# The second input load moved from SyncE's DMA queue to ScalarE's at the start of a depthwise-separable convolution kernel

## The chip, the cores and the metric

The kernel runs on one core of a Trainium2 chip. The metric is the device time of one execution in microseconds (us); lower is better. TensorE does the matmuls, VectorE and ScalarE move and convert data, GpSimd does a few small copies, and SyncE issues most of the DMAs. DMAs of SyncE and of ScalarE stand in two queues of their own, q1 and q10 in the profile.

## The reference

The inputs are x (1, 384, 384, 384) in bf16, a depthwise filter dw (1, 1, 384) and a pointwise matrix pw (384, 384). With a filter of one tap the padding is zero, and what is computed is a scaling of each channel and a matrix product:

```python
out = x * dw[0, 0][None, None, None, :]
return jnp.einsum('bhwc,cd->bhwd', out, pw)
```

So the kernel multiplies 147,456 rows of 384 channels by one 384 x 384 matrix whose rows have been scaled by dw. It reads and writes about 113 MB each.

## The kernel before, in words

**Tiling.** The rows are cut into 288 *supertiles* of 512 rows. Supertiles are loaded in *chunks*: the first five chunks hold 1, 1, 2, 2 and 4 supertiles, then 26 chunks hold 10 each, and the last ones get small again. A chunk t is loaded by one DMA, `load_x(t)` (line 134), and x0, x1, x2 in the text are the chunks 0, 1, 2. The loads of a chunk of one supertile have 384 KB. Chunks belong to groups (the first five are group 0), and each group uses one of three input buffers `Xs` in turn. Each of the first five chunks has a place of its own in the first buffer, and a semaphore of its own (`s_x[0][0]` to `s_x[0][4]`), so the first five loads wait for nothing.

**What is done to a supertile.** VectorE transposes it in two halves into a buffer T (line 365): for each half it does one 32 x 32 block transpose of pairs of bf16. TensorE then does 48 matmuls of 32 rows by 384 columns (line 226, in four row groups at the same time) into four PSUM banks `PS[s]`, and ScalarE copies the four banks to an output buffer O (line 425). SyncE stores the outputs (line 174). There are two T buffers and two sets of PSUM banks, used in turn.

**Weights, at the start.** `pw` is loaded by SyncE in two DMAs (lines 181 and 182: rows 0 to 127, then rows 128 to 383). ScalarE's queue loads `dw_row` (line 179) and, in `touched` (line 180), four bytes of every fourth row of x0. TensorE turns dw into a column and multiplies pw by selection matrices that hold it (line 276, k = 0, 1, 2, two results r each, the two of k = 2 with some matmuls repeated). The six results are converted to `w_r` by casts (line 381): the second by VectorE, the five others by ScalarE. TensorE runs some matmuls on constants before and between (line 243). The matmuls of line 226 begin when three of ScalarE's casts and VectorE's one are done, and the first half of x0 is transposed:

```python
w_first = {(0, 0): [(0, 1), (1, 3)], (4, 0): [(1, 4)], (4, 1): [(1, 5)]}
```

ScalarE's own order at the start is: issue `dw_row`, issue `touched`, load its activation table and write two small `warm` copies (line 342, they also release the two PSUM sets for the first time), then the casts, then the output copies.

**Order of the DMAs on SyncE.** It is written out by a sorted list `todo`, in which each entry has the supertile after which it is due; loads of the first three groups have -1 and come at once, in the order of the chunks. Before chunk 5 (the first one of 10 supertiles) SyncE waits until x1 has landed, and before the first store it has 28 waits that are long fulfilled. The semaphore `s_x` of a chunk is raised by its DMA whatever queue issued it, and VectorE waits for it before the first transpose of the chunk.

Of the kernel before, what the change touches and what calls it, by code (L numbers as in the profile page):

```python
# [26 lines left out]
def kernel(  # L27
# [12 lines left out]
    nc = tc.nc  # L40
# [19 lines left out]
    NT = len(chunks)  # L60
# [53 lines left out]
    with tc.tile_critical(sync_engine=mybir.EngineType.Pool, no_gpsimd_drain=True):  # L114
        def x_of(t):
            g, i, off, first, L = chunks[t]
            if first + 2 == NS:
                return Xl[:], s_xl, 32
            n = sum(len(ls) > i for ls in groups[g % NR : g + 1 : NR])
            return Xs[g % NR][:, 4 * off : 4 * (off + L), :], s_x[g % NR][i], 16 * n  # L120

        def load_x(t, eng=nc.sync):
            g, i, off, first, L = chunks[t]
            dst, sem, _ = x_of(t)
            rows = xf[512 * first : 512 * (first + L), :]
            if first + 3 < NS:
                src = rows.rearrange("(p s) c -> p (s c)", p=P)
                dst = dst.rearrange("p s c -> p (s c)")
                if i == 0 and g >= NR:
                    je = g_end[g - NR]  # L130
                    eng.wait_ge(s_t[je % 2][1], je // 2 + 1)
            else:
                src = rows.rearrange("(a k q) c -> q a k c", k=4, q=4)
            eng.dma_start(dst, src).then_inc(sem, 16)
# [46 lines left out]
        nc.sync.dma_start(pw_n[:, 0], pw[0:P, :]).then_inc(s_pw, 16)  # L181
        nc.sync.dma_start(pw_n[:, 1:3], pw[P:C, :].rearrange("(k p) d -> p k d", p=P)).then_inc(s_pw2, 16)
        load_x(0)

        todo = []
        for t, (g, i, off, first, L) in enumerate(chunks):
            if 0 < t < NT - 2:
                todo.append((g_end[g - NR] if g >= NR else -1, load_x, (t,)))
            for k in range(n_parts[t] - (first + 1 == NS)):
                todo.append((first + L * (k + 1) // n_parts[t] + 1, store, (t, k)))  # L190
# [275 lines left out]
```

## Time and profile before

| | |
|---|---|
| median of 4 runs | 573.96 us (573.54 to 574.03) |
| the profiled execution, its own time | 575.26 us |
| span of the profiled execution, first to last instruction | 573.2 us |
| mean granted TensorE clock | 0.999 |
| TensorE busy | 568.0 us (99%) |
| VectorE busy, ScalarE busy | 507.4 us (89%), 418.8 us (73%) |
| DMA queue of SyncE (q1) | 25796 packets, 225.91 MB, 97.5% of 16 engines' span |
| DMA queue of ScalarE (q10) | 1078 packets, 0.89 MB, 0.5% |

The span runs from the first to the last instruction of the profiled execution. Rows of the profile give a line of the kernel, an engine, an operation, its output and input, and a count; then the busy time, the mean duration of one in ns, and the idle time of the engine just before it with what ended that idle time. In the timeline each row begins with its start and its duration in us. An engine with "q" behind its name (SPq, ACTq) is the queue in which it issues DMAs; such a row is the issue, not the transfer. The time of a transfer is given as "us to landing", from the start of its issue.

### The profile page before, as it was taken

Reading aid. Unit: us, or ns where it says so; the run is one execution under the profiler, and the core shown is the slowest. Engines: PE = TensorE matmul, PEld = TensorE weight load, DVE = VectorE, ACT = ScalarE, POOL = GpSimd, SP = SyncE. Lnnn points to the kernel's source line nnn. Section 1 sums busy time; section 2 is a strip of 40 time slices with the busy share of each in tenths; the row PEclk is TensorE's granted clock in tenths of the full one; section 3 lists DMA queues with packets and bytes.
Section 4 is the critical chain, followed back from the end, with each engine's and each line's share of the span. In section 5 each row is a group of like instructions: output and inputs, shape, how many; then the busy total and the mean of one; then the engine's idle time right before and its main releaser. Section 6 shows DMA issues by size and latency. Waiting matters only on the chain.

```text
span 573.2 us, 29707 instructions
## 1 busy us (share of the span) xinstructions
PE 568.0 (99%) x13843; PEld 383.5 (67%) x13843; DVE 507.4 (89%) x586; ACT 418.8 (73%) x298; POOL 13.9 (2%) x41
## 2 busy tenths in 40 slices
PE   8999999999999999999999999999999999999997
PEld 4666666666666666666666666666666666666664
DVE  6898889889889889988988988988898898898885
ACT  6777777777777777777777777777777777777775
POOL 2042000000000000000000000000000000000000
PEclk9999999999999999999999999999999999999999
DMA  8999999999999999999999999999999999997877
GB/s 325 440 391 425 420 417 426 441 415 414 420 416 397 388 398 426 402 389 401 426 400 383 416 415 406 390 420 412 393 399 426 398 386 404 420 396 303 338 288 262
DMA packets 26884, 226.88 MB, mean 396 GB/s; under 512 B 1529, under 2 KB 7418, under 8 KB 23034
## 3 DMA queue, kind: packets, MB, share of 16 engines
q1 hardware_dynamic: 25796, 225.91, 97.5%
q10 hardware_dynamic: 1078, 0.89, 0.5%
q14 instruction: 9, 0.07, 0.0%
q8 instruction: 1, 0.02, 0.0%
HBM read 113.54 MB, written 113.25 MB: 396 GB/s over the span
## 4 chain that ended last, share of the span: by engine, by line
PE 99%; DMA 1%; ACT 0%; issue 0%; SPq 0%; POOLq 0%
PE ps L226 98%; DMA raw<-in_pw_dram 1%; PE ps L276 0%; PE ps L311 0%; PE ps L299 0%; ACT O L420 0%; SPq L181 0%; SPq L461 0%; POOLq L114 0%; POOLq L450 0%
## 5 line engine op out<-in xcount | busy, mean ns | idle before, releaser
L226 PE MATMUL ps<-w_r,T 32*128 32x384 bf16 x13776 | 560.8, 322 | 0.1
L365 DVE STREAM_TRANSPOSE T<-X 128x384 uint32<-128x384 uint32 x572 | 500.1, 875 | 57.4 <-DMA X<-in_x_dram 2.0
L425 ACT CAST O<-ps 128x1536 bf16<-128x1536 f32 x286 | 411.7, 1440 | 147.4 <-PE ps L226 147.4
L226 PEld LDWEIGHTS ps<-w_r,T 32*128 32x128 bf16 x13776 | 380.6, 93 | 180.6 <-issue 0.7
L340 POOL COPY Xk<-Xl 32x256 bf16<-32x256 bf16 x16 | 6.3, 394 | 0.0
L339 POOL COPY Xk<-Xl 32x128 bf16<-32x128 bf16 x16 | 4.6, 287 | 24.4 <-DMA Xl<-in_x_dram 23.5
L381 ACT CAST w_r<-ps 128x768 bf16<-128x768 f32 x5 | 3.7, 810 | 0.9 <-PE ps L276 0.9
L334 POOL COPY raw<-w_r 32x768 bf16<-32x768 bf16 x4 | 3.3, 819 | 6.9 <-ACT w_r L381 6.8
L276 PE MATMUL ps<-raw 64*128 64x384 bf16 x16 | 2.9, 516 | 0.5 <-DMA raw<-in_pw_dram 0.4
L243 PE MATMUL ps<-const-bfloat16-1.0 32*128 32x384 bf16 x24 | 2.2, 515 | 1.1 <-PEq L450 1.1
L342 ACT ACT_TABLE_LOAD x1 | 1.3, 1283 | 1.9 <-issue 1.9
L276 PEld LDWEIGHTS ps<-raw 64*128 64x128 bf16 x16 | 0.9, 126 | 2.5 <-DMA raw<-in_pw_dram 1.9
L416 DVE CAST O<-ps 128x384 bf16<-128x384 f32 x2 | 1.0, 552 | 1.4 <-PE ps L226 1.4
L365 DVE STREAM_TRANSPOSE T<-Xl 128x384 uint32<-128x384 uint32 x2 | 1.7, 872 | 0.2
L243 PEld LDWEIGHTS ps<-const-bfloat16-1.0 32*128 32x128 bf16 x24 | 0.7, 117 | 1.4 <-issue 1.4
L353 DVE STREAM_TRANSPOSE T<-Xk 128x384 uint32<-128x384 uint32 x2 | 1.2, 578 | 0.5 <-PE ps L226 0.4
L386 DVE TENSOR_REDUCE sel<-eye 128x64 f32<-128x128 bf16 x1 | 0.3, 289 | 1.5 <-POOL eye L321 1.5
L311 PE MATMUL ps<-raw,T 128*128 128x384 bf16 x8 | 1.5, 328 | 0.0
L420 ACT CAST O<-ps 128x384 bf16<-128x384 f32 x2 | 1.0, 478 | 0.7 <-PE ps L311 0.7
L381 DVE CAST w_r<-ps 128x768 bf16<-128x768 f32 x1 | 1.0, 958 | 0.5 <-PE ps L276 0.5
L420 DVE CAST O<-ps 128x384 bf16<-128x384 f32 x2 | 1.1, 558 | 0.1
L415 ACT CAST O<-ps 128x384 bf16<-128x384 f32 x2 | 0.9, 482 | 0.5 <-PE ps L226 0.5
(13 smaller groups left out, 4.5 us busy)
## 6 DMA issues: line engine op xcount, KB each, us to landing
X<-in_x_dram SPq DMA_DIRECT2D x26, 3840.0 KB, 21.3
out_dram<-O SPq DMA_DIRECT2D x26, 3840.0 KB, 27.3
X<-in_x_dram SPq DMA_DIRECT2D x3, 1536.0 KB, 18.0
out_dram<-O SPq DMA_DIRECT2D x4, 768.0 KB, 7.5
out_dram<-O SPq DMA_DIRECT2D x2, 1536.0 KB, 13.0
X<-in_x_dram SPq DMA_DIRECT2D x1, 2304.0 KB, 19.6
out_dram<-O SPq DMA_DIRECT2D x1, 2304.0 KB, 10.6
X<-in_x_dram SPq DMA_DIRECT2D x4, 384.0 KB, 4.7
```

What stands on the lines that cost most here:

```text
L226: mm = nc.tensor.matmul(PS[s][:, q, :D], lhsT=Ts[s][32 * q : 32 * q + 32, b, par::2], rhs=w_r[32 * q : 32 * q + 32, b, par, :], start=(b, ...
L243: nc.tensor.matmul(PS[0][:, 2 * (i % 2) + i // 2, :D], lhsT=ones[32 * i : 32 * i + 32, 0:P], rhs=ones[32 * i : 32 * i + 32, :], start=True ...
L276: mm = nc.tensor.matmul(PS[(k + 1) % 2][:, 2 * r + v, :D], lhsT=sel_w[64 * v : 64 * v + 64, k, r, :, :].rearrange("p q w -> p (q w)"), rhs ...
L311: mm = nc.tensor.matmul(PS[1][:, m, :D], lhsT=Tk[:, P * (m + 2) : P * (m + 3), par], rhs=w_k[:, par, :], start=False, stop=par == 1,)
L334: nc.gpsimd.tensor_copy(w_k[quads[n]], w_r[quads[n], n]).then_inc(s_wk)
L339: nc.gpsimd.tensor_copy(Xk[quads[n], g:8:4, :], x_b).then_inc(s_xk)
L340: nc.gpsimd.tensor_copy(Xk[quads[n], 8 + g : 24 : 4, :], Xl[quads[g], :, 64 * n : 64 * n + 64]).then_inc(s_xk)
L342: nc.scalar.copy(warm[:, s : s + 1], nc.const_aps.tensor(0.0, [P, 1], F32)).then_inc(s_a[s])
L365: ins = nc.vector.transpose(out=Tw[:, 3 * h : 3 * h + 3], in_=Xw[:, :, j, 96 * h : 96 * h + 96].rearrange("p k (b w) -> p b k w", w=32),)
L381: o = nc.vector.tensor_copy(out, in_) if e == 0 else nc.scalar.copy(out, in_)
L420: o = (nc.scalar.copy if n % 2 else nc.vector.tensor_copy)(Ov[:, n, j, :], PS[s][:, n, :D])
L425: a = nc.scalar.copy(Ov[:, :, j, :], PS[s][:, :, :D])
```

## The change

The load of chunk 1 is taken out of the sorted list on SyncE and issued on ScalarE, as its third instruction of the kernel, behind `dw_row` and `touched` and ahead of the table load. `load_x` already has the engine as an argument. The destination, the source and the semaphore are the same.

```diff
         load_x(0)
+        load_x(1, nc.scalar)
 
         todo = []
         for t, (g, i, off, first, L) in enumerate(chunks):
-            if 0 < t < NT - 2:
+            if 1 < t < NT - 2:
                 todo.append((g_end[g - NR] if g >= NR else -1, load_x, (t,)))
```

## The prediction

> **What bounds the kernel now.** I read the page's engine and chain parts first, then the chain in order of time, because its start shows what the change can touch. From the page:
>
> ```profile
> span 573.2 us, 29707 instructions
> ...
> PE 568.0 (99%) x13843; PEld 383.5 (67%) x13843; DVE 507.4 (89%) x586; ACT 418.8 (73%) x298; POOL 13.9 (2%) x41
> ...
> PE 99%; DMA 1%; ACT 0%; issue 0%; SPq 0%; POOLq 0%
> ...
> L226 PE MATMUL ps<-w_r,T 32*128 32x384 bf16 x13776 | 560.8, 322 | 0.1
> L365 DVE STREAM_TRANSPOSE T<-X 128x384 uint32<-128x384 uint32 x572 | 500.1, 875 | 57.4 <-DMA X<-in_x_dram 2.0
> ```
>
> TensorE is the bound. Its main line, L226, runs 560.8 us and stood idle 0.1 us in all. VectorE waited for x in 2.0 us only, three times (the waits table), all in the first 10 us. So x is never late for TensorE, and the change can act only on when the L226 run starts, on how fast its first microseconds go, and on the tail. Next, the chain in order of time:
>
> ```profile
> 1.41 3.16 DMA raw<-in_pw_dram
> 4.58 0.05 issue
> 4.62 2.10 PE ps L276 x12
> 6.72 0.08 issue
> 6.81 560.81 PE ps L226 x13189
> ```
>
> The start at 6.81 hangs on the second weight load (pw rows 128 to 383), not on x. Then the timeline of the first 8 us (start, duration):
>
> ```profile
> 0.96 0.54 ACTq L179 DMA_DIRECT2D dw_row<-in_dw_dram  x1
> 1.53 0.37 ACTq L180 DMA_DIRECT2D touched<-in_x_dram  x1
> 1.88 1.41 SPq L134 DMA_DIRECT2D X<-in_x_dram  x3
> 1.93 1.28 ACT L342 ACT_TABLE_LOAD   x1 [1.93 <-issue]
> 3.23 0.28 ACT L342 COPY warm<-const-float32-0.0 128x1 f32<-128x1 f32 x2
> 3.91 0.80 ACT L381 CAST w_r<-ps 128x768 bf16<-128x768 f32 x1 [0.39 <-PE ps L276]
> 5.16 1.50 ACT L381 CAST w_r<-ps 128x768 bf16<-128x768 f32 x2 [0.46 <-PE ps L276]
> 5.53 1.04 DVE L365 STREAM_TRANSPOSE T<-X 128x384 uint32<-128x384 uint32 x2 [0.34 <-DMA X<-in_x_dram]
> 7.06 1.04 DVE L365 STREAM_TRANSPOSE T<-X 128x384 uint32<-128x384 uint32 x2 [0.50 <-DMA X<-in_x_dram]
> ```
>
> L226 needs three ScalarE casts of weights; the third ends at 5.16 + 1.50 = 6.66, and TensorE starts 0.15 later. It also needs the first transposed half of x0: x0 lands about 5.5, half of 1.04 later it is 6.05. So x0 has about 0.6 us of slack. x1 is transposed from 7.06, its first half ready at 7.6. TensorE needs it after the first supertile, near 9.9 (ScalarE's first output cast starts at 9.97). So x1 has 2.3 us to spare: getting it earlier buys nothing by itself.
>
> **What the Trainium skill says.** "DMA: Bandwidth & Descriptors", section "Issuing engines are not separate DMA queues": transfers issued by different engines run on the same 16 DMA engines and interleave; only issue time is saved. Section "Queues, rings and completion order" of the same page: each engine goes round robin between its queues. The trace agrees as far as it shows. In the window 3.41 to 3.70 us, while both queues had work:
>
> ```profile
> q1 hardware_dynamic: 63, 0.08, 107.3%
> q10 hardware_dynamic: 62, 0.00, 12.0%
> ```
>
> 63 packets of SyncE's queue and 62 of ScalarE's (the tiny "touched" reads) went in the same 0.29 us. ScalarE's queue did not wait for SyncE's. "TensorE: Matmul & The Clock Gate", Part 1: matmuls run at half clock until a busy window of about 3.4 us has passed. The trace agrees: L226 matmuls take 516 ns on average in the window 6.8 to 8.1 and 321 ns in 9.3 to 11.0, with the first short ones near 8.8.
>
> **The change, part by part.**
>
> *SyncE.* One issue goes: three issues took 1.41, so 0.47 each, and x2, x3 and x4 are issued 0.47 sooner. They remain behind x0 in SyncE's queue, and the total bytes ahead of x2's end are the same, so x2 lands where it did (transposed from 9.24, needed near 9.9 + 1.95 = 11.9). x5 still waits on SyncE for x1, 2.7 us in the trace. It can move by about 0.5 either way, hidden by x4 ahead of it, 1536 KB issued near 1.88 + 4 × 0.47 = 3.8 and landing 11.5 later. Stores come after 11.4. Cost 0.
>
> *ScalarE.* One issue is added between "touched" and the table load. No row shows this issue on ScalarE early; its neighbours are 0.37 to 0.54, and the late ScalarE load of the same 384 KB takes 0.65. I take 0.4. Then the table load starts at 2.3, the warm copies end at 3.9, and the first weight cast starts at about 3.95 for 3.91. That cast ends at 4.75; the next one waits for TensorE until 5.16. The slack is 0.39 before the first cast plus 5.16 − 4.71 = 0.45 after it: 0.84 in all. At 0.4 the cost is 0; at 0.65 still 0. Queued behind the issue are the table load, the two copies that release PSUM, and the casts; no new semaphore wait is added.
>
> *DMA, the second weight load.* It lands at 4.57. x1 would be issued at 1.93, and x0, issued at 1.88, moves its first packets at about 3.4 (of the 125 packets in the window above, 109 are under 2 KB, so 16 are x0's). In 3.88 to 4.22 the trace has 15 packets under 2 KB, 6 of them under 512 B: 9 weight packets still to go. A 3 KB packet of x1 takes 3072 B at 396/16 = 24.8 GB/s, 0.124 us. If each of the nine were held up by one, the delay is 1.1; if x1 arrives after them, 0. "touched" takes the first five turns, so I take 0.3.
>
> *DMA, x0.* Alone in the queue it lands at 1.88 + 3.6 = 5.5; x1 follows at about 7.05, so a load of this size takes 1.0 (at 396 GB/s) to 1.5. Interleaved from the start, x0 ends nearly where the pair ends: later by 0 (x1 arrives late) to 1.5 (x1 wholly ahead). I take 1.0. Its first half is then transposed at 7.05, TensorE starts at about 7.2, and x0 has become the last wait. x1 lands near 6.8 or before and is queued on VectorE behind x0's transposes, ready near 8.1: in time.
>
> *Sum.* Start = the later of weights (6.81 + 0.3) and x0 (6.66 + 0.4 + 0.15): 0.4 later. While TensorE is at half clock until about 8.8 whatever it does, a late start of 0.4 loses work worth only 0.2; if the clock's rise moves along, 0.4. I take **0.3**. The profiled execution's span is 573.2 (its own time 575.26, 1.3 above the median), so the span after would be about 573.5; the median 573.96 becomes **574.3**. The end is not touched: the last stores follow the last matmuls.
>
> **Rivals.**
>
> *No change (573.9 to 574.1).* The change need not make the loads run side by side: x1's packets are behind "touched", and if descriptors for the two queues are made one after the other, x0 is nearly through first. For it: x0's slack of 0.6 and the weights' earlier issue. Against it: the equal packet counts above.
>
> *Clock not raised (slower, 576.0).* In the stretch from 2.0 to 5.4 TensorE waited 0.43 for the second weights and stayed at half clock; in 5.4 to 8.8 it waited 0.09 before L226 and the clock rose. If x0 becomes late by more than its slack, that gap grows to about 0.4, as long as the one that went with a cold clock. If the rise then fails, another window of 3.4 us runs at half rate (rows every 0.32 for 0.16), and costs half of it: 1.7, plus 0.3. It decides from the point where x0 lands later than about 6.2. Against it: if the weights are late by as much, the gap falls before the matmuls of L276 and not behind them.
>
> *ScalarE becomes the bound (slower, 574.8 to 575.1).* An issue of x on SyncE took up to 1.97 (the maximum of line 134; its median is 0.35). Such an issue on ScalarE, 1.1 past the slack of 0.84, shifts every weight cast by 1.1: 0.6 to 1.1. Against it: the first issues of x in this trace are short.
>
> *Faster (573.0).* Only 293 GB/s flowed in 3.4 to 5.5. If two queues fill this better, or if the clock rises earlier by a shift of its window, the gain is at most the half-clock part of L226: 6.81 to 8.8, half of 2.0, 1.0. Nothing in the change brings the weights sooner.
>
> **How the numbers follow.** 0.2% is 1.15 us, about what a measurement of this kernel can tell from no change. Likeliest case 0.53 (574.0 to 574.9), no change 0.20, clock 0.14, ScalarE 0.07, faster 0.06. Slower by over 0.2% is all of the clock case, half of ScalarE's and a tail of the likeliest, 0.20; faster by over 0.2%, 0.04, since its ceiling is 1.0; the rest, 0.76, is the same. The range 573.2 to 576.0 leaves out the larger half of the clock case and the faster case, some 0.13, and the bounds of x0 (to 1.5) and weights (to 1.1) fit in it.
>
> **What would show it.** ScalarE's queue has a third early issue of about 0.4 and the table load starts near 2.3; SyncE's L134 run has one issue fewer. x0's transposes start near 6.5 for 5.53 and x1's directly behind. The second weights' matmuls start 4.6 to 4.9, L226 near 7.1 to 7.2. The third cast still ends by 7.0. The first short L226 matmul is near 8.8; near 12 it is the clock case. I am wrong if L226 starts at 6.8 or before, if it has idle time past its start, or if the median moves by over 1.15 with the start where I put it.

## The result and the profile after

The change made the kernel slower by about 0.1%: the median went from 574.09 us (63 runs) to 574.63 (42 runs), and the ratio of the times is 1.0013 with a 95% interval of 1.0007 to 1.0018, so 0.4 to 1.0 us. That is below the 0.2% at which the prediction drew its line, and beyond what noise explains. The profiled execution took 574.53, with a span of 572.4.

The single times say more than the median. Of the 63 runs of before, 11 lie over 575.0; of the 42 after, 17 do. Below 575.0 the medians are 574.06 and 574.49, so 0.43 apart; of the 17 upper times of after, 13 lie between 575.9 and 577.3, some 1.7 above the lower ones. The means, which count the upper times in full, are 574.36 and 575.09, so 0.73 apart. So two things changed: all executions became a little later, and a second cluster of times became more frequent. The experiments look for a cause of each.

The page after, engines and the costliest group:

```profile
span 572.4 us, 29707 instructions
...
PE 566.2 (99%) x13843; PEld 417.1 (73%) x13843; DVE 507.4 (89%) x586; ACT 418.3 (73%) x298; POOL 13.9 (2%) x41
...
L227 PE MATMUL ps<-w_r,T 32*128 32x384 bf16 x13776 | 559.8, 321 | 1.2 <-DVE T L366 1.2
```

All lines below the added one are one higher now: L226 has become L227. Its idle time went from 0.1 to 1.2 us, and what ended it is VectorE's transpose. All of that wait lies ahead of its first matmul. The chain in order of time says the same:

```profile
1.88 4.39 DMA X<-in_x_dram
6.27 0.02 issue
6.29 0.59 DVE T L366
6.88 0.09 issue
6.97 559.83 PE ps L227 x13776
```

In place of the weight load, the load of x0 now heads the chain. The timeline of the same execution:

```profile
1.93 0.44 ACTq L134 DMA_DIRECT2D X<-in_x_dram  x1
2.41 1.28 ACT L343 ACT_TABLE_LOAD   x1 [2.41 <-issue]
...
3.91 0.80 ACT L382 CAST w_r<-ps 128x768 bf16<-128x768 f32 x1
...
4.42 1.32 PE L277 MATMUL ps<-raw 64*128 64x384 bf16 x12 [0.23 <-DMA raw<-in_pw_dram]
6.29 1.96 DVE L366 STREAM_TRANSPOSE T<-X 128x384 uint32<-128x384 uint32 x4 [1.10 <-DMA X<-in_x_dram]
```

ScalarE's table load is 0.48 later and its first cast still at 3.91, as forecast. x0's transposes start at 6.29, and x1's follow with no wait between. In the window 3.9 to 5.5 us the two queues share the DMA engines about evenly (packets, MB, share of the 16 engines' time):

```profile
q10 hardware_dynamic: 100, 0.31, 56.1%
q1 hardware_dynamic: 103, 0.28, 44.6%
```

One trap: the span fell from 573.2 to 572.4, while the kernel became slower. The profiled execution of before (575.26) was one of its upper times, the one after was a lower one. Two single profiles can't be subtracted as they stand, and the experiments therefore begin with what a usual execution of before looks like.

### The profile page after: what moved, and what is told of

Read it like the earlier page. It is cut to its first block, busy times and chain, and to the rows that moved or that the text cites. A ratio compares the mean times of both kernels' runs of the same rounds, so it can differ in the third digit from the quotient of the medians.

```text
span 572.4 us, 29707 instructions
## 1 busy us (share of the span) xinstructions
PE 566.2 (99%) x13843; PEld 417.1 (73%) x13843; DVE 507.4 (89%) x586; ACT 418.3 (73%) x298; POOL 13.9 (2%) x41
## 4 chain that ended last, share of the span: by engine, by line
PE 98%; DMA 1%; SPq 0%; DVE 0%; issue 0%; ACT 0%; POOLq 0%
PE ps L227 98%; DMA X<-in_x_dram 1%; PE ps L312 0%; PE ps L300 0%; DVE T L366 0%; ACT O L421 0%; SPq L182 0%; SPq L181 0%; SPq L462 0%; POOLq L114 0%; POOLq L451 0%
## 5 line engine op out<-in xcount | busy, mean ns | idle before, releaser
L227 PE MATMUL ps<-w_r,T 32*128 32x384 bf16 x13776 | 559.8, 321 | 1.2 <-DVE T L366 1.2
L227 PEld LDWEIGHTS ps<-w_r,T 32*128 32x128 bf16 x13776 | 414.6, 93 | 146.5 <-issue 1.6
```

The costliest lines, as they stand in the source:

```text
L227: mm = nc.tensor.matmul(PS[s][:, q, :D], lhsT=Ts[s][32 * q : 32 * q + 32, b, par::2], rhs=w_r[32 * q : 32 * q + 32, b, par, :], start=(b, ...
```

## The experiments

Theories. **Sharing**: x0 lands late because x1's packets take turns with its own, and TensorE waits for x0. Rivals: **issue**, that the added DMA issue ahead of ScalarE's table load costs; **queue**, that a load on ScalarE's queue costs by being there. For the upper times: **clock**, that TensorE's half clock goes on for another window when it idles too long ahead of its main matmuls, against **late transfer**, that in these executions some load comes later still.

| kernel | x0's transposes start | main matmuls start | full clock from | its own time | median us (runs) | over 575.0 |
|---|---|---|---|---|---|---|
| before, first profile | 5.53 | 6.81 | 8.86 | 575.26 | 574.09 (63) | 11 |
| before, second profile (e5_before) | 5.72 | 6.40 | 7.20 | 574.25 | 574.07 (13) | 2 |
| the change | 6.29 | 6.97 | 4.78 | 574.53 | 574.63 (42) | 17 |
| the change, e9_look1 | 6.28 | 6.96 | 10.91 | 576.40 | | |
| the change, e9_look2 | 6.20 | 6.88 | 5.79 | 574.55 | | |
| e2_issue | 5.36 | 6.38 | 4.82 | 573.86 | 573.83 (21) | 1 |
| e3_x1_first | 7.40 | 8.08 | 6.01 | 575.55 | 576.33 (11) | 9 |
| e1_apart | 6.25 | 6.93 | 6.14 | 575.34 | 575.84 (7) | 7 |
| e4_apart2 | 5.37 | 6.29 | 6.86 | 573.73 | 574.30 (14) | 2 |
| e6_fill | 6.37 | 7.05 | 5.08 | 574.38 | 574.75 (22) | 10 |
| e8_fill128 | 6.64 | 7.32 | 6.46 | 574.88 | 574.44 (13) | 3 |
| e7_nofill | 5.59 | 6.27 | 9.33 | 575.15 | 574.47 (14) | 5 |
| e10_before_fill | 5.44 | 6.68 | 6.60 | 574.54 | 574.19 (13) | 0 |

Columns two to five are of one profiled execution, which can be a slow or a quick one of its kernel; the last two are of all its runs. "Full clock from" is where the one long full-speed stretch begins in the trace's record of the granted clock. The record has no entry ahead of that stretch, so the page's PEclk doesn't show the half clock at the start. Each group of runs had runs of the kernel before beside it, and the ratios are against these. Over 575.0 were 11 of 63, 5 of 34, 3 of 51, 0 of 17 and 1 of 17 of them, so shares of different groups have to be compared with care.

**What a span is made of.** Take from a span the start of the main matmuls and half of the time from there to full clock. In eleven of the thirteen profiles 565.4 to 565.6 us are left: 572.42 − 6.97 in the change, 572.27 − 6.40 − 0.40 in the second profile of before, 574.33 − 6.96 − 1.98 in e9_look1. The other two (e1_apart, e10_before_fill) have a gap later in the main matmuls, of 0.42 at 11.0 and of 0.46 at 26.4. So in the profiles of the change the start and the clock are the whole loss, and a rival has to act through one of them.

**A usual execution of before.** The kernel is unchanged.

> The kernel before, unchanged, for a second profile. Clock theory: the first profile of it (its own time 575.26) had a late second weight load and a late rise of the clock, and is one of the few upper times. A usual execution (574.0) has its second weights by 4.4, x0's transposes directly behind VectorE's cast near 5.3, L226 starting at 6.4 to 6.6 and no long L226 matmul. Rival: it looks as the first profile does, start at 6.8 and long matmuls until 8.8.

The timeline of TensorE and of VectorE in this second profile (574.25 us, span 572.3):

```profile
3.37 2.94 PE L276 MATMUL ps<-raw 64*128 64x384 bf16 x16
...
6.40 5.92 PE L226 MATMUL ps<-w_r,T 32*128 32x384 bf16 x132
...
5.72 1.04 DVE L365 STREAM_TRANSPOSE T<-X 128x384 uint32<-128x384 uint32 x2 [0.53 <-DMA X<-in_x_dram]
```

The second weights came in time: the sixteen matmuls of L276 have no row of their own for a wait. The main matmuls start at 6.40, and only the first few are long: the group of L226 has a mean of 476 ns in the window 6.3 to 7.2 and 335 in 7.2 to 10. So the first profile, with its start at 6.81 and long matmuls until 8.9, was an upper one, and the start to compare with is 6.4. Two expectations were not met: that of no long matmul at all, and that of x0 directly behind VectorE's cast near 5.3; its transposes waited for x0 until 5.72. The main matmuls start 0.68 behind that, just as in the change (6.97 − 6.29), so in this execution x0 had no slack left.

**The issue alone.** x1 stays on SyncE; ScalarE issues a third tiny load where the change has x1's issue.

```diff
+    touched2 = consts.tile([P, 2], BF16, name="touched2")
 ...
         load_x(0)
+        nc.scalar.dma_start(touched2[:], xf[0 : 4 * P : 4, 0:2]).then_inc(s_to, 16)
 ...
-        nc.sync.wait_ge(s_to, 16)
+        nc.sync.wait_ge(s_to, 32)
```

> The kernel before (x1 on SyncE) with a third small DMA on ScalarE where the change puts x1's issue: 128 reads of 4 bytes, as in the touched load, so an issue of about 0.4 us and almost no traffic. Sharing theory: table load near 2.4, first weight cast still near 3.91, x0 at 5.5, no change in time (within 0.3 us of the kernel before). Rival, the issue ahead of the table load is what costs: 0.4 to 0.8 us slower than before.

Ratio 0.9996 (0.9989 to 1.0002). Timelines of ScalarE and TensorE:

```profile
1.93 0.44 ACTq L185 DMA_DIRECT2D touched<-in_x_dram  x1
2.40 1.28 ACT L344 ACT_TABLE_LOAD   x1 [2.40 <-issue]
...
6.38 1.81 PE L228 MATMUL ps<-w_r,T 32*128 32x384 bf16 x40 [0.51 <-ACT w_r L383]
```

The issue took 0.44 as in the change and moved the table load as far, and the main matmuls started at 6.38. The issue rival falls.

**x1 ahead of x0 in one queue.**

```diff
+        load_x(1)
         load_x(0)
-        load_x(1, nc.scalar)
```

> Both loads on SyncE's queue, but x1 ahead of x0. Nothing added on ScalarE. Sharing theory: x0 has the whole of x1 ahead of it in place of about half, so it lands near 7.0 (where x1 landed before), L226 starts near 7.7, and the time is 0.8 to 1.1 us over the kernel before, about twice the cost of the change; TensorE idles about 1.9 us before L226. Rival, the cost comes from ScalarE's issue or queue: no worse than before by more than 0.3.

Ratio 1.0035 (1.0020 to 1.0049). Timeline of VectorE and TensorE:

```profile
7.40 1.96 DVE L366 STREAM_TRANSPOSE T<-X 128x384 uint32<-128x384 uint32 x4 [2.21 <-DMA X<-in_x_dram]
...
8.08 1.16 PE L227 MATMUL ps<-w_r,T 32*128 32x384 bf16 x24 [1.85 <-DVE T L366]
```

With nothing added on ScalarE, the kernel loses more than by the change. The start is 8.08 − 6.40 = 1.7 late, three times the 0.57 of the change; the wait of 1.85 is where it was expected. The median is 2.2 over that of before beside it (574.09). I had expected 0.8 to 1.1 us, because I reckoned from the first profile's start at 6.81 and had x0 at 7.0. The times run from 574.66 to 578.08; how much of this spread is the clock isn't shown, since the one profile had full clock from 6.01.

**x1 on ScalarE's queue, but apart from x0: first version.** The issue was written between the two warm copies, and SyncE waits for x0 before x2.

```diff
-        load_x(1, nc.scalar)
+        nc.sync.wait_ge(x_of(0)[1], 16)
 ...
             nc.scalar.copy(warm[:, s : s + 1], ...).then_inc(s_a[s])
+            if s == 0:
+                load_x(1, nc.scalar)
```

> x1 stays on ScalarE's queue, but is issued between the two warm copies (about 1.4 us later than in the change), and SyncE issues x2 only when x0 has landed, so that neither moves beside x0. Sharing theory (x0 lands late because x1's packets take turns with its own): x0's transposes start near 5.5 again for 6.29, L226 starts near 6.6 with the third weight cast as its last wait, and the median is that of the kernel before within 0.3 us. Rival, ScalarE's issue or its queue costs something by itself: the time stays 0.4 to 0.8 us above the kernel before. x1 must be transposed by about 8.5 or a wait for it is added.

Ratio 1.0026 (1.0015 to 1.0037), but this version did not do what it was made for. ScalarE's timeline:

```profile
1.93 1.28 ACT L343 ACT_TABLE_LOAD   x1 [1.93 <-issue]
1.99 0.38 ACTq L134 DMA_DIRECT2D X<-in_x_dram  x1
```

ScalarE issued the DMA while the table load was still running, at 1.99 for 1.93 in the change. So x1 was beside x0 again, and x0's transposes started at 6.25. That separates one thing after all: the table load was back at 1.93 and the loss stayed. SyncE's wait added a loss of its own by making x2 late; TensorE's timeline has a gap there:

```profile
9.70 1.32 PE L227 MATMUL ps<-w_r,T 32*128 32x384 bf16 x28
11.44 0.83 PE L227 MATMUL ps<-w_r,T 32*128 32x384 bf16 x16 [0.42 <-issue]
```

**Second version.** A wait on ScalarE's sequencer holds the issue back; x2 waits for the second weights only.

```diff
-        load_x(1, nc.scalar)
+        nc.sync.wait_ge(s_pw2, 16)
 ...
             nc.scalar.copy(warm[:, s : s + 1], ...).then_inc(s_a[s])
+            if s == 1:
+                nc.scalar.wait_ge(s_pw, 16)
+                load_x(1, nc.scalar)
```

> x1 on ScalarE's queue, but ScalarE issues it behind the warm copies and a wait for the first weight load (landed near 3.3), so near 3.4 in place of 1.9; SyncE issues x2 behind a wait for the second weight load (near 4.3), so that x2 does not overtake x1. x0 then has moved most of its packets before x1's begin (near 4.9). Sharing theory: x0's transposes start by 5.5, L226 starts near 6.4, and the time is that of the kernel before within 0.3 us. Rival, a load on ScalarE's queue costs by being there, whenever it is issued: L226 starts near 6.9 as in the change, 0.4 to 0.8 us over the kernel before.

Timelines of ScalarE, VectorE and TensorE:

```profile
3.02 0.33 ACTq L134 DMA_DIRECT2D X<-in_x_dram  x1
...
5.37 1.04 DVE L369 STREAM_TRANSPOSE T<-X 128x384 uint32<-128x384 uint32 x2 [0.18 <-DMA X<-in_x_dram]
6.87 1.04 DVE L369 STREAM_TRANSPOSE T<-X 128x384 uint32<-128x384 uint32 x2 [0.47 <-DMA X<-in_x_dram]
...
6.29 1.90 PE L227 MATMUL ps<-w_r,T 32*128 32x384 bf16 x36
```

Issued 1.1 later, on the same queue, x1 leaves x0 alone: x0 is back at 5.37 and the start at 6.29, where the queue rival expected 6.9. The times alone would not decide. The ratio of 1.0005 (0.9996 to 1.0013) allows both no loss and that of the change, the median is 0.33 over that of before beside it (573.97), and the profiled execution (573.73) is one of the fastest of its 14; why the usual one is later isn't shown. What decides is the landing of x0 in all profiles: its transposes start at 6.20 to 6.64 in the six in which x1 moves beside it, at 7.40 with x1 ahead of it, and at 5.36 to 5.72 in the six in which x1 comes behind or later. So the queue rival falls, and on the first part the runs settle it: sharing.

**The upper times: fill the gap.** The change, with matmuls on constants while TensorE waits for x0. First with two row groups of 32:

```diff
+        nc.tensor.wait_ge(s_wr[1], 2)
+        for _ in range(5):
+            for i in (0, 1):
+                nc.tensor.matmul(
+                    PS[0][:, i, :D],
+                    lhsT=ones[32 * i : 32 * i + 32, 0:P],
+                    rhs=ones[32 * i : 32 * i + 32, :],
+                    start=True,
+                    stop=True,
+                    tile_position=(32 * i, 0),
+                )
         with nc.tensor.Fori(0, NS // 2 - 1, 1) as it:
```

> The change, with five more rounds of two matmuls each on constants between L276 and L226, behind ScalarE's second cast of weights, so that TensorE idles about 0.4 in place of 1.2 us while it waits for x0. Their results are overwritten. Clock theory (the gap lets the half clock last another window in part of the executions): times over 575.0, 17 of 42 for the change, become one in four or fewer, where the fill ends late they lie up to 0.5 higher. Rival, the upper times come from DMA: their share stays near 40%.

Ten of 22 times lie over 575.0, as in the change; the ratio is 1.0018 (1.0010 to 1.0026). By that run alone the clock theory would have fallen, though the gap in its profile had shrunk to 0.35. But that profile had full clock from 5.08. Where the clock is still low, five rounds take about 1.6 us (an estimate, from the 0.32 between the weight loads of L276 at half clock in the first profile of before), end near 7.9 and are a late start of their own, so not each of the ten times need be a late clock. Then with whole-array matmuls of the same number of rounds:

```diff
+        nc.tensor.wait_ge(s_wr[1], 2)
+        for _ in range(5):
+            nc.tensor.matmul(PS[0][:, 0, :D], lhsT=ones[:, 0:P], rhs=ones[:], start=True, stop=True)
```

> The change, with five matmuls of all 128 rows on constants in the place of the ten 32-row ones, so that the whole array is busy while TensorE waits for x0. Their results are overwritten. If a gap ahead of L226 makes the upper times and the 32-row fill was too thin to count as busy: times over 575.0 fall to one in five or fewer, the median to 574.4 to 574.6. If the gap has nothing to do with it: their share stays near 40%, as with the thin fill (10 of 22).

Three of 13 times lie over 575.0, a little more than the one in five that was expected. The highest is 575.25, and none is in the cluster near 576: over 575.7, a line drawn after the runs, the change has 13 of 42 and the thin fill 6 of 22. If the share were the same, none in 13 would come about once in 60 times beside the change, and once in 20 beside the thin fill. TensorE's timeline:

```profile
3.37 2.95 PE L277 MATMUL ps<-raw 64*128 64x384 bf16 x16
6.25 1.08 PE L288 MATMUL ps<-const-bfloat16-1.0 128*128 128x384 bf16 x5
7.32 1.97 PE L227 MATMUL ps<-w_r,T 32*128 32x384 bf16 x44
```

The gap is gone. The fill did not bring x0 sooner; its transposes start at 6.64 here and the main matmuls at 7.32, but this execution took 574.88, so it is a late one. The median is 574.44 and the ratio 1.0006 (0.9998 to 1.0014), an interval that overlaps that of the change. The run supports the clock theory; it doesn't prove it by itself.

**Two more profiles of the change.** The kernel is that of the change.

> The change, unchanged, for another profile. Its times are 574.0 to 574.8 in 25 of 42 runs and 575.1 to 577.2 in 17. If this one is an upper one, then by the clock theory L226 starts near 7.0 and its matmuls are long (520 ns) for 3 us or more of its first 5 us; by the rival (a late transfer) they are short from the start and L226 starts near 8.5 or has a gap. If it is a lower one: L226 from about 7.0, short matmuls from 8.1 at the latest.

> As the look before it: the change, unchanged, for one more profile. Upper time: long matmuls for 3 us or more by the clock theory, a late start or a gap in L226 by the rival; lower time: L226 from about 7.0 and short matmuls from 8.1 at the latest.

The first has an upper time, 576.40; the second a lower one, 574.55. In the first one TensorE's timeline starts the main matmuls like this:

```profile
6.96 2.43 PE L227 MATMUL ps<-w_r,T 32*128 32x384 bf16 x28 [0.64 <-DVE T L366]
```

and in the second one:

```profile
6.88 2.43 PE L227 MATMUL ps<-w_r,T 32*128 32x384 bf16 x53 [0.76 <-ACT w_r L382]
```

The starts are 0.08 apart, and in the same 2.43 us one execution does 28 matmuls and the other 53. The groups by shape in the window 7.0 to 10.5, first of the upper time,

```profile
L227 PE MATMUL ps<-w_r,T 32*128 32x384 bf16 x48 | 4.0, 519 | 0.6 <-DVE T L366 0.6
```

then of the lower one:

```profile
L227 PE MATMUL ps<-w_r,T 32*128 32x384 bf16 x92 | 3.9, 321 | 0.8 <-ACT w_r L382 0.8
```

No transfer is late in the upper one; x0's transposes start at 6.28 in it and at 6.20 in the other. Its last long matmul ends at 10.99, and the record has full clock from 10.91. From 6.96 to there at half speed is 3.95 us, which costs half, 1.98; the two times are 1.85 apart. So this upper time is the clock, and no late transfer. It is the only upper time of the change with a profile; the two others whose full clock comes after 8 us, the first profile of before (575.26) and e7_nofill (575.15), are upper times too. The two remaining ones over 575.0 (e3_x1_first, e1_apart) have full clock by 6.2 and are slow by their start or a gap.

**The other way round: less to do at the start.** The kernel before without the matmuls on constants at its head.

```diff
-        idle_work(4)
 ...
-        idle_work(2)
```

> The kernel before without the six rounds of matmuls on constants (L243) at its start; loads, casts and transposes are as they were. Clock theory: TensorE becomes busy about 2 us later, L276 runs at half clock throughout, long L226 matmuls are seen in the profile, and most times lie in the upper part: median 0.7 to 1.7 over the kernel before. Rival, the upper times come from DMA: median within 0.3 and the same share of upper times (about one in six).

The profiled execution has the long matmuls that the clock theory wants, with full clock from 9.33; groups by shape in the window 6.3 to 9.0:

```profile
L226 PE MATMUL ps<-w_r,T 32*128 32x384 bf16 x36 | 3.1, 518 | 0.1
```

Five of 14 times are over 575.0, against 3 of 51 of before beside it. But the median rose by 0.5 only, for an expected 0.7 to 1.7, and the ratio, 1.0005 (0.9995 to 1.0014), leaves no change possible. The share fits the clock theory, the size was over-estimated, and by its time the run is inconclusive.

**A fill for the kernel before.** One whole-array matmul in its shorter gap.

```diff
+        nc.tensor.wait_ge(s_wr[1], 2)
+        for _ in range(1):
+            nc.tensor.matmul(PS[0][:, 0, :D], lhsT=ones[:, 0:P], rhs=ones[:], start=True, stop=True)
         with nc.tensor.Fori(0, NS // 2 - 1, 1) as it:
```

> The kernel before with one matmul of all 128 rows on constants between L276 and L226, behind ScalarE's second cast of weights; at half clock it takes 0.32 us, about the gap of the second profile of before (6.28 to 6.40, with 0.2 more of the array idle). Its result is overwritten. Clock theory: the few upper times of before (over 575.0 in 19 of 165 runs so far) that come from this gap go, those from a late second weight load stay; median within 0.2 us of before, ratio 0.999 to 1.000. Rival: the fill delays L226 where the clock is low, 0.1 to 0.2 slower.

Ratio 1.0000 (0.9991 to 1.0008); no time is over 574.54, against one of 17 over 575.0 beside it. With so few upper times in before, 13 runs can't show whether the share fell. No version here is shown to beat the kernel before.

## Why the prediction was right, point by point

- **The place.** Right: the change acts on the start of the main matmuls alone. After it L227 has no idle time but the wait ahead of its first matmul, and the end is untouched: start and clock account for the span, with the same 565.4 to 565.6 left in before and after.
- **ScalarE's issue.** Right: 0.44 for 0.4, the table load at 2.41 for 2.3, the first cast unmoved, cost 0. The issue by itself is 0.9996 of before.
- **SyncE.** Right: nothing is lost by x2 to x5 in the change.
- **The second weights.** Mis-sized: 0.3 was taken, and no loss shows. TensorE could load them from 4.02 to 4.42 in the three profiles of the change, and from 4.03 and 4.62 in the two of before. In the profile after, x1's first 3 KB packet starts at 3.86, when five of the 384 weight packets were left.
- **x0.** The mechanism is right, shown from both sides by e3_x1_first and e4_apart2. Its size, 1.0, was too large: the transposes start at 6.20 to 6.29 in the three profiles of the change and at 5.53 to 5.72 in the two of before, 0.5 to 0.8. Its slack of 0.6 was too large as well. It was read from an execution with late weights; in the second profile of before there was none, in e2_issue and e4_apart2, with x0 at 5.36 and 5.37, about 0.3.
- **The sum.** 0.3 was forecast, 0.54 measured by the medians. The delay of the start was forecast as 1.0 less 0.6, so 0.4, to 7.2; measured against the start of a usual execution it is 6.97 − 6.40 = 0.57. That 0.4 and 0.57 are near each other is in part luck, since two sizes that were too large cancel. And I charged half of it because the first profile had a low clock until 8.8; in ten of the thirteen profiles the clock is full by 4.8 to 7.2, and a delay behind that costs its whole length. Among the lower times it cost 0.43.
- **The signs.** The table load and x1's transposes behind x0's came as described. The start lay a little ahead of the 7.1 to 7.2 given, and the first short main matmul came with the start, at 6.97, not near 8.8.
- **The clock rival.** I gave it as a case beside the likeliest, with a chance of 0.14. It is not an alternative but a share of the executions: 17 of 42 after, where the runs of before have 11 of 63. That the clock rises a window late is shown by the first of the two further profiles; that the gap ahead of the main matmuls is what delays it is supported by the whole-array fill and by the busy shares given at the end, not isolated by a run. Its price, 1.7, is about the distance of the cluster. What I argued against it did not hold, since in that profile x0 was late and the second weights were not.
- **No change, ScalarE as the bound, faster.** None of them occurred.

## What to carry to other kernels

A second queue gave no second set of DMA engines: the load that was needed first got about half of them while the other moved beside it (103 and 100 packets in 1.6 us). With both loads in one queue their order was a priority, and splitting gave it away. Ask which landing is the next one on the chain before issuing anything beside it. And where a kernel starts with a cold matmul clock, look at the distribution of times, not at one profile: here an idle gap of 0.64 us came with a loss of 1.85 in one execution, and with a larger share of such executions.

## What the runs showed of the hardware

- The trace's record of the granted clock shows one full-speed stretch of 566.61 us in most profiles and of 563.20 in three: the first one of before (575.26), the upper one of the change (576.40), and e7_nofill (575.15). The difference, 3.41 us, is the window that the Trainium skill gives ("TensorE: Matmul & The Clock Gate", Part 1).
- Counted back from the rise in steps of 3.41 us, the windows of the thirteen profiles part by how busy TensorE was: 0.89 or more of each window that ended with the rise, 0.85 or less of each one before it. In the upper profile of the change it was 0.85 (0.67 to 4.08), then 0.81 (4.08 to 7.50, with the gap in it), then all. So with these kernels a window with about half a microsecond of idle time kept the clock low. The ends of matmuls are modelled in the trace, and no run sets the limit on purpose.
- Filling the gap with matmuls on two 32-row groups did not lower the share of upper times (10 of 22); with 128-row matmuls none of 13 was near 576. Whether the part of the array in use counts is not shown.
- ScalarE issued a DMA that stands behind a table load and a copy in its program while the table load still ran: at 1.99 with the table load from 1.93 to 3.21 (e1_apart). A semaphore wait held it back, and even then it came at 3.02, ahead of the copies at 3.23 (e4_apart2). Ahead of the table load in the program, the issue of 0.44 moved the load from 1.93 to 2.41.
